# Moving three groups of instructions in the later pairs of a fused attention and gated feed-forward kernel: subtractions on VectorE, copies on ScalarE, one small layer on TensorE

## The chip, the cores and the metric

The kernel runs on one core of one Trainium2 chip. TensorE (PE in the profile) multiplies matrices into PSUM, VectorE (DVE), ScalarE (ACT) and GpSimd (POOL) work element by element, and SyncE (SP) issues most of the transfers between HBM and the on-chip memory SBUF. [...] The metric is the device time of one execution in microseconds (us), as the median of several runs; lower is better.

## The reference

Eight sequences of 512 tokens and 32 states go through a two-way attention, and its output goes through a feed-forward block whose activation is h times cos(h). Everything is float32.

```python
def _attn_ref(x, state):                       # x (8, 8, 512, 64), state (8, 8, 32, 64)
    scale = 1.0 / np.sqrt(D)
    a = softmax(scale * np.matmul(x, state.transpose(0, 1, 3, 2)))
    xread = np.matmul(a, state)
    a2 = softmax(scale * np.matmul(state, x.transpose(0, 1, 3, 2)))
    sread = np.matmul(a2, x)
    return np.concatenate([xread, sread], axis=2)

def _moe_ref(x, w_in, w_out):                  # x (4352, 512), w_in (512, 2048), w_out (2048, 512)
    h = x @ w_in
    g = h * np.cos(h)
    return g @ w_out
```

The row of tokens of a sequence times w_in is never formed as written: since xread is a times state, the kernel first makes state times w_in (the "state products", 32 rows for each head) and then multiplies the attention weights a by that.

## The kernel before, in words

The work is a list of steps, one for each tile of 128 hidden columns: 16 steps (NF) for each of the eight sequences b, and at the end 16 more steps for the states of all sequences together (b = 8, called the states' tiles). Two sequences form a pair of 32 steps (PERIOD). The first pair is placed by a small planner with costs and due times; from step 32 on the order is written out by hand, one call of `later_pair` for each step, and only that part is touched here. Tiles are handled two at a time: an even step and the odd step behind it share one PSUM bank pair `h`.

For a later pair, the hidden tile h of step + 2 is made from the attention weights and the state products with seven half-sized products in place of eight: `seven_part` with k = 0 to 3 (PE, line 543; two parts in each step), sums of weights on POOL made three steps ahead (`sw_sums`, line 521), two copies on ACT after part 0 (`seven_copies`, lines 528 and 529) and two sums on DVE (`seven_sum`, line 551). For the states' tiles the hidden layer is one plain product, `hidden` (PE, line 488, eight matrix instructions). Then comes the activation: `gate` (ACT, line 564, rounds h), `gate2` (DVE, line 567), `gate3` (ACT, line 570, the sine), `gate4` (DVE, line 584, writes g into `g_all` and with that frees the `h` banks for the tile after the next).

The product g times w_out of a pair is likewise done with seven products in place of eight at the outer level, named p1 to p7, and each of these again with seven inner stages (`Product.stage`, k = 0 to 6, PE line 772, eight matrix instructions each). The outer level needs differences between the four quarters of g ("rows" 0 to 3): `outer_sum`, which calls `sub` (line 715) on DVE in pieces of 128x1024 or on POOL in pieces of 128x512. The inner level needs differences too: `Product.sums`, always POOL, also line 715. In an inner product, stage 1 writes the upper half of bank c; its `follow` copies the lower half of c into b and the upper half into a small buffer (ACT, lines 780 and 781). Stage 2 then goes on adding into the lower half of c. Which stages, sums and outer differences belong to which step is laid down in the tables `stage_at`, `sums_at` and `outer_at`; a step has one stage, an even step or the last of a period two, and the 15 states' steps from 129 on share the last 28 stages. In an even step the first of two stages stands in the middle of `later_pair`, the second at the step's end.

The attention of sequence b + 1 and the state products of b and b + 1 are laid into the steps of b by `plan(b)`, as lists `todo[0]` to `todo[5]` for each step s of the 16: `pe` (0), `x_act`, `y_act`, `x_dve`, `y_dve`, `z_act`. `go(n)` issues list n. State products are made in steps s = 0, 3, 8 and 12 (PE, line 312) into the two PSUM banks `at`, and copied out by ACT (`products_kept`, line 462, two copies). In step s = 4 the scores of sequence b + 1 (PE, line 312 again) are written into the same two banks `at`; sequences 3 to 7 have such a step inside the part that is touched.

Below, the pairs are numbered 0 to 3; the outer differences and most inner stages of a pair run in the first half of the pair behind it, those of pair 3 in the states' steps from 128 on.

Of the kernel before, what the change touches and what calls it, by code (L numbers as in the profile page):

```python
# [22 lines left out]
def kernel(  # L23
# [15 lines left out]
    NF = Dff // P  # L39
# [33 lines left out]
    def quad(n):  # L73
        return g_all[:, QT * n:QT * n + QT]
# [392 lines left out]
    def part(b, name, *args):  # L467

        if b not in attn:
            attn[b] = Attention(b)  # L470
        getattr(attn[b], name)(*args)
        if (name, args) == ("reads", (1,)) and b + 1 < B:
            if b > 0:
                attn[b + 1] = Attention(b + 1)
                loads_due.extend(attn[b + 1].load_tokens())
            loads_due.extend(load_x(b + 1))
# [5 lines left out]
    def hidden(t):  # L482
        if t.paired:
            t.hp = h_pairs[t.at][:, t.f % 2, 0:t.n]
        else:
            t.hp = single_pool.tile([P, S], F32, name="h1")
        for i in range(t.kn):
            nc.tensor.matmul(out=t.hp, lhsT=t.lhs(i), rhs=t.rhs(i),  # L488
                             start=(i == 0), stop=(i == t.kn - 1))
# [76 lines left out]
    def gate2(t):  # L566
        nc.vector.tensor_tensor(t.q, t.q.bitcast(I32), t.hp, op=ALU.subtract)  # L567
# [5 lines left out]
    def gate4(t):  # L573
        row = t.row
        if t.i // QT == len(quads_of[row]):
            quads_of[row].append(quads_free.pop(0))
        t.slot = QT * quads_of[row][t.i // QT] + t.i % QT
        t.g = g_all[:, t.slot, 0:t.n]
        g = t.g
        if t.paired:  # L580
            t.mate.slot = t.slot + 1
            t.mate.g = g_all[:, t.slot + 1, 0:t.n]
            g = g_all[:, t.slot:t.slot + 2, 0:t.n]
        nc.vector.tensor_tensor(g, t.hp, t.q, op=ALU.mult)  # L584
# [117 lines left out]
    def fetch_block(n):  # L702

        if n < len(stage_list):
            product_, k = stage_list[n]
            nc.sync.dma_start(
                out=ring[n % NB].rearrange("p i d -> p (i d)"),
                in_=blocks_kept[WEIGHTS[product_.name], ORDER[k]])

    def sub(engine, o, x1, x2):  # L710
        n = max(1, S // o.shape[2])
        if engine is nc.vector:
            n = o.shape[1]
        for i in range(0, o.shape[1], n):
            engine.tensor_tensor(o[:, i:i + n], x1[:, i:i + n], x2[:, i:i + n],  # L715
                                 op=ALU.subtract)
# [253 lines left out]
    warm(WARM, a0.xp[3])  # L970

    def plan(b):
        pe, x_act, y_act, x_dve, y_dve, z_act = [
            {s: [] for s in range(NF)} for _ in range(6)]

        def prod(s, b, nt, *bank):
            pe[s].append((b, "products", nt) + bank)
            x_act[s].append((b, "products_kept", nt) + bank)

        def pairs(s, b, name, kept, i):  # L980
            pe[s] += [(b, name, i), (b, name, i + 1)]
            x_act[s].append((b, kept, i))
            y_act[s].append((b, kept, i + 1))

        def early(b, s):
            for k in range(NK):
                to = (x_dve, y_dve)[k % 2]
                to[s[k // 2]].append((b, "tokens_turned", k))
            pe[s[2]].append((b, "scores"))
            x_dve[s[2]].append((b, "max1"))  # L990
            x_dve[s[3]].append((b, "spread1"))
            y_dve[s[3]].append((b, "shift"))
            y_dve[s[4] - 1].append((b, "max2"))
            z_act[s[4]].append((b, "exps"))
            y_dve[s[4]].append((b, "sums1"))
            x_dve[s[5]].append((b, "spread2"))
            y_dve[s[5]].append((b, "norm1"))

        def late(b, s):
            pairs(s[0], b, "turn", "turn_kept", 0)  # L1000
            pe[s[1]].append((b, "reads", 0))
            pe[s[2]].append((b, "reads", 1))
            x_dve[s[2]].append((b, "keep"))
            pe[s[3]].append((b, "keep2"))
            x_act[s[3]].append((b, "keep3"))

        if b:
            prod(0, b, 1)
            prod(3, b, 2)
            prod(8, b, 3)  # L1010
            if b + 1 < B:
                prod(12, b + 1, 0)
                early(b + 1, (1 + (b == 1), 2 + (b == 1), 4, 5, 7, 8, 9))
                late(b + 1, (9, 10, 11, 15))
        return pe, x_act, y_act, x_dve, y_dve, z_act


    all_tiles = list(tiles())
    for i, t in enumerate(all_tiles):
        t.mate = all_tiles[i ^ 1]  # L1020
    pairs = [all_tiles[2 * NF * n].pair for n in range(B // 2)]
    stage_at, sums_at, outer_at, weights_at = [
        defaultdict(list) for _ in range(4)]
# [25 lines left out]
    dve, pool = nc.vector, nc.gpsimd  # L1049
# [14 lines left out]
    def outer_sum(engine, n, o, x1, x2, half, i):  # L1064
        o, x1, x2 = [quad(quads_of[n, r][half])[:, 2 * i:2 * i + 2]
                     for r in (o, x1, x2)]
        sub(engine, o, x1, x2)
# [29 lines left out]
    def stages(step, n=100):  # L1097
        nonlocal n_stages
        later_copy = step % NF == 7
        copy = nc.vector.tensor_copy if later_copy else nc.scalar.copy  # L1100
        for pd, k in stage_at[step][0:n]:
            pd.stage(k, copy)
            n_stages += 1
            fetch_block(n_stages + NB - 2)
        del stage_at[step][0:n]
# [4 lines left out]
    def go(n):  # L1110
        for p in todo[n]:
            part(*p)
# [513 lines left out]
    def names_raw(i):  # L1626
        h = i % 2
        n = (2 * h, 2 * h + 1) if i < 4 else range(QT)
        return " ".join(f"Q{SLOTS[i]}_{k}" for k in n)

    def later_pair(step, t, ahead):
        coming = ahead[0] if ahead and ahead[0].paired else None
        seven_ = coming is not None and seven(coming)
        first = coming if even or coming is None else coming.mate
        if not t.paired:
            hidden(t)
        if even or not t.paired:
            gate(t)
        else:
            gate3(t.mate)  # L1640
            go(5)
        if seven_:
            seven_part(first, 0 if even else 2)
        elif coming is not None:
            hidden(coming)
        if even or not t.paired:
            gate2(t)
        if t.b == 1 and s in (13, 14):
            halves(2, s - 13)
        if seven_ and not even:  # L1650
            seven_sum(first, 1)
        if not t.paired:
            gate3(t)
        if not t.paired:
            gate4(t)
        elif not even:
            gate4(t.mate)
        if even:
            stages(step, 1)
        go(0)  # L1660
        if not even:
            stages(step, 1)
        if seven_:
            seven_part(first, 1 if even else 3)
            if even:
                seven_sum(first, 0)
        go(1)
        go(3)
        if t.pair is None and not even:
            state_sums(t.mate)  # L1670
            state_sums(t)
        go(2)
        go(4)

    first_pair()
    for step, t in enumerate(all_tiles[FIRST:], FIRST):
        s, even = step % NF, step % 2 == 0
        if s == 0 and t.b < B:
            steps = plan(t.b)
        todo = [p[s] if t.b < B else [] for p in steps]  # L1680
        while stores_due:
            stores_due.pop(0)()
        for u in all_tiles[step + 3:step + 4]:
            if seven(u) and u.f % 2 == 0:
                sw_sums(u)
        now[0] = step
        while totals_due and totals_due[0][0] <= step:
            totals_due.pop(0)[1]()
        if step == PERIOD:
            singles.__exit__(None, None, None)  # L1690
            pool2 = ctx.enter_context(tc.tile_pool(name="hps2", bufs=1,
                                                   space=PSUM))
            h_pairs[0] = pool2.tile([P, 2, S], F32, name="h2")
        later_pair(step, t, all_tiles[step + 2:step + 3])
        if later and later[0][0] <= step:
            later.pop(0)[1]()
        for what in weights_at[step]:
            what()
        for what in outer_at[step]:
            outer_sum(*what)  # L1700
        for pd, k in sums_at[step]:
            pd.sums(k)
        if t.b < B - 1 and t.b > 1 and s in (12, 13):
            halves(t.b + 1, s - 12)
        stages(step)
        load_now(H if step < NF else 4)
        if step == PERIOD * (B // 2) - 8:
            load_end_weights(2)
        if t.pair is None and t.n_th > 3 and len(quads_free) > 2:
            load_end_weights(1)  # L1710
# [36 lines left out]
```

## Time and profile before

| | value |
|---|---|
| time, median of 3 runs | 739.78 us (738.67 to 739.96) |
| the profiled execution's own time | 740.65 us |
| its span, first to last instruction | 738.9 us |
| mean granted TensorE clock | 0.993 |
| DVE busy | 506.8 us (69%) |
| ACT busy | 347.3 us (47%) |
| POOL busy | 542.5 us (73%) |
| DVE line 715, 128x1024, 42 of them | 62.0 us, 1490 ns each |
| POOL line 715, 128x512, 252 of them | 332.5 us, 1349 ns each |

The profile is of one execution. Its own time, 740.65 us, is 0.87 us above the median of the three timed runs, and 1.75 us above its span; a saving that is read from the trace is set against the first of these. Times inside the trace are counted from the first instruction. PE is busy almost throughout, so what counts is its short gaps and what ends them; an idle stretch of another engine matters only where PE waits behind it.

### The profile page before, as it was taken

What the parts mean: (1) busy time and instruction counts of PE and PEld (TensorE: products, weight loads), DVE (VectorE), ACT (ScalarE), POOL (GpSimd) and SP (SyncE); (2) the same over time, 40 slices, a digit from 0 to 9 for tenths busy, and PEclk for the clock granted to TensorE, in tenths of its full rate; (3) what the DMA queues carried; (4) which work ended last, traced back from release to release, by engine and by line L of the source; (5) the groups of instructions that cost most, each with busy time, mean ns of one, the idle gap of its engine ahead of it and who ended that gap; (6) DMA issues with size and microseconds to landing.
All of it is one profiled execution on the core that took longest, in us unless ns stands there. A gap on an engine that the chain in (4) does not pass through costs nothing.

```text
span 738.9 us, 10734 instructions
## 1 busy us (share of the span) xinstructions
PE 708.2 (96%) x3626; PEld 519.0 (70%) x3626; DVE 506.8 (69%) x703; ACT 347.3 (47%) x586; POOL 542.5 (73%) x524
## 2 busy tenths in 40 slices
PE   8898889999999999999999999999999999999997
PEld 3343343477778878777778788777688788888886
DVE  4989979957866668849756577768665467355550
ACT  5799675654463446343634464344634533211110
POOL 1557789375998997588998665879989665799600
PEclk9999999999999999999999999999999999999999
DMA  9966799536346964693238635762225466456662
GB/s 297 285 192 193 236 265 301 122 96 150 87 128 117 214 172 115 142 197 86 82 80 168 160 96 116 147 154 83 75 68 119 115 205 143 108 156 203 155 152 46
DMA packets 204021, 111.33 MB, mean 151 GB/s; under 512 B 149888, under 2 KB 166784, under 8 KB 203968
## 3 DMA queue, kind: packets, MB, share of 16 engines
q1 hardware_dynamic: 202880, 110.14, 57.4%
q8 instruction: 29, 0.48, 0.3%
q10 hardware_dynamic: 960, 0.39, 0.2%
q14 instruction: 24, 0.20, 0.1%
q0 software_dynamic: 128, 0.13, 0.1%
HBM read 87.03 MB, written 23.59 MB: 150 GB/s over the span
## 4 chain that ended last, share of the span: by engine, by line
PE 59%; POOL 21%; DVE 9%; issue 3%; DMA 3%; ACT 2%; SPq 1%; ACTq 0%; POOLq 0%; DVEq 0%
PE o L772 29%; POOL g_all L715 16%; PE h L543 13%; PE h L488 8%; POOL swS_all L521 3%; PE at L312 3%; PE at L877 2%; DMA held<-in_state_dram 2%; PE o L640 2%; POOL sw_all L521 2%; DVE g_all L715 1%; PE at L417 1%; DVE q_all L567 1%; DVE g_all L232 1%; DVE g_all L584 1%
## 5 line engine op out<-in xcount | busy, mean ns | idle before, releaser
L715 POOL TENSOR_TENSOR g_all<-g_all 128x512 f32<-128x512 f32 x252 | 332.5, 1349 | 61.8 <-DVE g_all L715 40.4
L772 PE MATMUL o<-g_all 128*128 128x256 f32 x1456 | 343.7, 381 | 2.4 <-POOL g_all L715 2.4
L772 PEld LDWEIGHTS o<-g_all 128*128 128x128 f32 x1456 | 273.7, 190 | 49.7 <-issue 5.7
L567 DVE TENSOR_TENSOR q_all<-q_all,h 128x1024 f32<-128x1024 int32 (+1 forms) x88 | 85.3, 971 | 40.7 <-ACT q_all L564 40.4
L564 ACT ACTIVATE q_all<-h 128x1024 int32<-128x1024 f32 (+1 forms) x88 | 73.1, 833 | 81.2 <-PE h L543 35.1
L584 DVE TENSOR_TENSOR g_all<-h,q_all 128x1024 f32<-128x1024 f32 (+1 forms) x88 | 85.7, 973 | 24.5 <-ACT q_all L570 23.6
L570 ACT ACTIVATE q_all<-q_all,halfpi 128x1024 f32<-128x1024 f32 (+1 forms) x88 | 84.2, 957 | 38.7 <-DVE q_all L567 38.5
L551 DVE TENSOR_TENSOR h<-h,sums_all 128x256 f32<-128x256 f32 x96 | 41.3, 430 | 77.5 <-PE h L543 60.2
L488 PE MATMUL h<-aT_all,sw_all 128*128 128x512 f32 x128 | 64.0, 628 | 13.0 <-DVE g_all L584 12.3
L543 PE MATMUL h<-aT_all,sw_all 128*128 128x256 f32 x192 | 59.6, 392 | 3.8 <-DVE g_all L584 3.4
L543 PE MATMUL h<-aS_all,swS_all 128*128 128x256 f32 x192 | 60.2, 395 | 2.6 <-ACT sums_all L529 1.8
L715 DVE TENSOR_TENSOR g_all<-g_all 128x1024 f32<-128x1024 f32 x42 | 62.0, 1490 | 0.1
L543 PE MATMUL h<-aS_all,sw_all 128*128 128x256 f32 x192 | 58.0, 384 | 0.1
L488 PEld LDWEIGHTS h<-aT_all,sw_all 128*128 128x128 f32 x128 | 23.2, 195 | 44.3 <-issue 21.5
L521 POOL TENSOR_TENSOR swS_all<-sw_all 128x128 f32<-128x128 f32 x48 | 22.5, 468 | 41.8 <-ACT sw_all L462 41.8
L543 PEld LDWEIGHTS h<-aS_all,swS_all 128*128 128x128 f32 x192 | 33.9, 189 | 27.0 <-issue 12.1
L780 ACT COPY o<-o 128x256 f32<-128x256 f32 x26 | 9.3, 357 | 85.1 <-PE o L772 85.1
L543 PEld LDWEIGHTS h<-aT_all,sw_all 128*128 128x128 f32 x192 | 34.5, 189 | 16.3 <-DVE g_all L584 12.2
L237 POOL TENSOR_TENSOR w_in<-w_in,aS_all 128x1024 int32<-128x1024 int32 (+1 forms) x10 | 22.3, 2241 | 29.9 <-DVE w_in L232 27.2
L787 ACT COPY o<-sums_all 128x256 f32<-128x256 f32 x26 | 9.8, 378 | 68.2 <-PE o L772 68.2
L543 PEld LDWEIGHTS h<-aS_all,sw_all 128*128 128x128 f32 x192 | 35.6, 190 | 8.2 <-DVE h L551 2.7
L607 DVE SCALAR_TENSOR_TENSOR held<-o,held 128x512 f32<-128x512 f32 x38 | 25.9, 681 | 13.7 <-PE o L772 13.1
(116 smaller groups left out, 931.6 us busy)
## 6 DMA issues: line engine op xcount, KB each, us to landing
g_all<-blocks_kept SPq DMA_DIRECT2D x206, 256.0 KB, 2.8
blocks_kept<-g_all SPq DMA_DIRECT2D x48, 256.0 KB, 3.9
g_all<-in_moe_w_out_dram SPq DMA_DIRECT2D x8, 1024.0 KB, 5.7
out_dram<-ot SPq DMA_DIRECT2D x128, 64.0 KB, 2.0
g_all<-in_moe_w_in_dram SPq DMA_DIRECT2D x6, 1024.0 KB, 7.1
x_b<-in_x_dram SPq DMA_DIRECT2D x24, 256.0 KB, 4.7
xT<-in_x_dram SPq DMA_DIRECT2D x80, 64.0 KB, 2.8
x_b<-in_x_dram SPq DMA_DIRECT2D x16, 128.0 KB, 4.3
```

The source lines that it names most:

```text
L237: nc.gpsimd.tensor_tensor(bits, bits, e, op=ALU.add)
L488: nc.tensor.matmul(out=t.hp, lhsT=t.lhs(i), rhs=t.rhs(i), start=(i == 0), stop=(i == t.kn - 1))
L521: nc.gpsimd.tensor_tensor(o, x1, x2, op=op)
L543: nc.tensor.matmul(out=out_, lhsT=w, rhs=r, start=start, stop=True, skip_group_check=True)
L551: nc.vector.tensor_tensor(o, h2[:, LO], sums_all[:, 0], op=ALU.add)
L564: nc.scalar.activation(t.q.bitcast(I32), t.hp, func=ACTF.Copy, bias=0.25)
L567: nc.vector.tensor_tensor(t.q, t.q.bitcast(I32), t.hp, op=ALU.subtract)
L570: nc.scalar.activation(t.q, t.q, func=ACTF.Sin, bias=halfpi, scale=-TWO_PI)
L584: nc.vector.tensor_tensor(g, t.hp, t.q, op=ALU.mult)
L607: nc.vector.scalar_tensor_tensor(out=out.t[:, ch], in0=bank, scalar=TWO_PI, in1=b.t[:, ch], op0=ALU.mult, op1=ALU.add)
L715: engine.tensor_tensor(o[:, i:i + n], x1[:, i:i + n], x2[:, i:i + n], op=ALU.subtract)
L772: nc.tensor.matmul(out=o, lhsT=ring[(self.first + k) % NB][:, i], rhs=g[:, i], start=(start and i == 0), stop=(i == QT - 1), skip_group_ch ...
```

## The change

Three edits, all in steps from 32 on.

The copies of the state products made in an odd step (only s = 3) go into a new list `w_act` of the step behind it and are issued by `go(6)`, which stands after `gate` and `seven_part(first, 0)` with its two copies. They were issued in step s = 3 itself, ahead of the next step's `gate`. This happens once for each of the sequences 2 to 7, in steps 35, 51, 67, 83, 99 and 115 (copies in 36, 52, 68, 84, 100 and 116).

In steps whose next tiles are states' tiles, and whose first two stages are stages 1 and 2 of a product, stage 1 is issued ahead of `hidden`, so that the layer stands between the two stages. It stood ahead of both. This holds in steps 126, 133 and 137.

Outer differences on DVE that read or write row 3 and are due in an even step are kept back in `sums_late` and issued in the odd step behind it, after `gate4`. They were issued at the end of the even step. In each of pairs 0, 1 and 2 this moves one difference of the third step of the half (34, 66, 98) to 35, 67, 99 and one of the fifth (36, 68, 100) to 37, 69, 101; in pair 3 both differences of step 130 go to 131 and one of 132 to 133.

```diff
-        pe, x_act, y_act, x_dve, y_dve, z_act = [
-            {s: [] for s in range(NF)} for _ in range(6)]
+        pe, x_act, y_act, x_dve, y_dve, z_act, w_act = [
+            {s: [] for s in range(NF)} for _ in range(7)]
 
         def prod(s, b, nt, *bank):
             pe[s].append((b, "products", nt) + bank)
-            x_act[s].append((b, "products_kept", nt) + bank)
+            (w_act[s + 1] if s % 2 else x_act[s]).append(
+                (b, "products_kept", nt) + bank)
...
-        return pe, x_act, y_act, x_dve, y_dve, z_act
+        return pe, x_act, y_act, x_dve, y_dve, z_act, w_act
...
+    sums_late = []
+
     def later_pair(step, t, ahead):
...
         if seven_:
             seven_part(first, 0 if even else 2)
         elif coming is not None:
+            if [k for _, k in stage_at[step][0:2]] == [1, 2]:
+                stages(step, 1)
             hidden(coming)
         if even or not t.paired:
             gate2(t)
+        go(6)
         if t.b == 1 and s in (13, 14):
             halves(2, s - 13)
...
         elif not even:
             gate4(t.mate)
+            while sums_late:
+                outer_sum(*sums_late.pop(0))
         if even:
             stages(step, 1)
...
         for what in outer_at[step]:
-            outer_sum(*what)
+            if even and what[0] is dve and 3 in what[2:5]:
+                sums_late.append(what)
+            else:
+                outer_sum(*what)
```

The number of instructions on every engine and every transfer stays the same.

## The prediction

> **What bounds the kernel now.** I read the page first, then the waits of PE behind the first pair, then the chain of waits of one stretch, then the timeline around each gap. From the page, the span and the engines' busy shares, and PE in 40 slices:
>
> ```profile
> span 738.9 us, 10734 instructions
> ...
> PE 708.2 (96%) x3626; PEld 519.0 (70%) x3626; DVE 506.8 (69%) x703; ACT 347.3 (47%) x586; POOL 542.5 (73%) x524
> ...
> PE   8898889999999999999999999999999999999997
> ```
>
> The reader is to see that PE sets the pace; a change can gain only what PE stands idle. The waits of PE from 176 us on (who waited for whom: total, times, longest, in us):
>
> ```profile
> PE h L543 <- DVE g_all L584: 3.4, 8, 0.4
> PE o L772 <- POOL g_all L715: 2.4, 3, 0.8
> PE h L543 <- ACT sums_all L529: 1.8, 4, 0.5
> PE h L543 <- POOL swS_all L521: 0.8, 3, 0.3
> ```
>
> These 8.4 us are nearly all that any reordering can win. But not all of it is free, as the chain of waits of the stretch 332 to 376 us shows (start, length, what):
>
> ```profile
> 333.27 1.12 DVE g_all L715
> ...
> 334.45 6.88 POOL g_all L715 x4
> ...
> 350.43 9.82 POOL g_all L715 x8
> ...
> 362.15 10.84 POOL g_all L715 x8
> ...
> 372.99 0.42 POOL swS_all L521
> ...
> 373.45 0.70 PE h L543 x2
> ```
>
> POOL works here without a break from 334.45 to 373.4 (38.47 us busy of 39.00 in the table of windows), and PE then waits 0.27 us for its sum of weights. The same stretch begins at 176.75 and at 491.96, once for each of pairs 0 to 2. It is started by a difference on DVE in the pair's first step, which isn't moved, so PE can't pass its end earlier than now, however much it saves inside.
>
> [...] the four POOL sums from 334.45 take 6.88 us where four undisturbed ones take 4.96 (at 624.18), and the 128x128 sums at 342.36 and 343.63 take 1.31 and 1.44 us under the DVE pair at 341.91 where 0.46 is usual. So each DVE difference costs POOL about 0.95 us wherever it lies in the stretch. [...]
>
> **The change part by part**, against the profiled execution's 740.65 us.
>
> *States' layer between two stages (steps 126, 133, 137).* The timeline at 623 us:
>
> ```profile
> 623.01 1.89 PE L772 MATMUL o<-g_all 128*128 128x256 f32 x8
> ...
> 624.93 0.36 ACT L780 COPY o<-o 128x256 f32<-128x256 f32 x1 [2.43 <-PE o L772]
> 625.20 0.38 ACT L781 COPY sums_all<-o 128x256 f32<-128x256 f32 x1
> ...
> 625.68 1.97 PE L772 MATMUL o<-g_all 128*128 128x256 f32 x8 [0.78 <-POOL g_all L715]
> ```
>
> Stage 1 ends, ACT copies, and only then stage 2 starts. From start to start the matrix instructions follow at 0.216 us; over this gap it is 1.163, so 0.947 is lost, and another 0.075 at the next one: 1.02 us. It is the same at 661.80 and 681.82. The releaser is named as a POOL sum, but that sum writes what stage 2 doesn't read; the copies end 0.10 us ahead of PE's start, so I take them. Either way `hidden` (8 x 0.216 = 1.73 us of PE) now lies between and covers the 0.8 us of copies. Stage 1 starts 1.73 us earlier: its sums ended at 612.76 (needed 621.3), 651.58 and 673.18 (needed about 658 and 678), and its weights landed 5 us or more before. `hidden` itself comes later, but its banks were freed at 620.88 and its result is read two steps on. The moved orders of DVE (stage 2's sum ahead of other work) and SP (same order) hurt nobody. Gain 3 x 1.02 = 3.06; from below 2.0, if other small waits take a third. I take 3.0. Nothing else stalls PE after 626 us, so it reaches the end.
>
> *Copies behind the seven products, sequences 3 and 5 (steps 52 and 84).* The timeline at 263 us:
>
> ```profile
> 263.27 1.07 ACT L462 COPY sw_all<-at 128x512 f32<-128x512 f32 x2
> ...
> 264.21 1.06 ACT L564 ACTIVATE q_all<-h 128x1024 int32<-128x1024 f32 x1
> ...
> 265.13 0.41 ACT L528 COPY h<-h 128x256 f32<-128x256 f32 x1
> ...
> 265.57 0.37 ACT L529 COPY sums_all<-h 128x256 f32<-128x256 f32 x1
> 265.64 0.18 PEld L312 LDWEIGHTS at<-xT,st_all 64*32 64x32 f32 x16 [0.33 <-ACT h L528]
> ```
>
> The scores at 265.64 overwrite the two banks that the copies read. With the gate first: gate 263.27 to 264.2, the two copies of h to 265.0, then the two moved copies, the second ending at about 265.97. The second score instruction goes to that bank, so PE waits to about 266.1 (0.14 us from an ACT end to PE's start, as at 581.02 to 581.16): 0.47 us lost, and behind the waiting PE stands all of the step. PE had no wait near here that the earlier gate could remove, and POOL has idle time until the next pair, so nothing takes it back. Two steps: +0.94; bounds 0.6 and 1.4 (0.3 and 0.7 each).
>
> *The same, sequence 7 (step 116).* No scores follow, and here PE did wait for the copy of h:
>
> ```profile
> 580.65 0.37 ACT L529 COPY sums_all<-h 128x256 f32<-128x256 f32 x1
> ...
> 581.16 0.67 PE L543 MATMUL h<-aS_all,swS_all 128*128 128x256 f32 x2 [0.38 <-ACT sums_all L529]
> ```
>
> The copy ends 0.94 us earlier, and the loss of 0.54 us (start to start) is gone: -0.5; bounds -0.54 and 0.
>
> *The same, sequences 2, 4 and 6, with DVE's differences (steps 34 to 37, 66 to 69, 98 to 101).* The difference at 338.11 (2.09 us, part of it waiting for POOL) leaves the place ahead of gate4, which then ends at about 340.1 where it ended at 341.99; PE's loss of 0.28 at 342.05 goes. Three differences in a row follow gate4, and gate2 behind them starts at 344.1 to 344.7 as before. The moved copies then end at about 344.72, and the scores, due at 344.56, wait 0.26. The difference at 348.65 moves behind gate4, which ends 0.97 earlier; the loss of 0.59 at 352.23 goes. Together PE would be 0.6 us ahead. But it then waits at the sum of weights of 373.40, behind the unbroken POOL stretch, into which the same three differences fall with the same 0.95 us each. [...] So the 0.27 of idle time there becomes about 0.8, and three pairs give 3 x -0.1 = -0.3; bounds +0.2 and -0.6 each.
>
> *Differences of pair 3 (steps 130 and 132).* DVE has gaps of 1 to 5 us there and POOL's sums are used 5 us or more after they end: 0.
>
> Sum: -3.0 + 0.94 - 0.5 - 0.3 = -2.9, say -2.8 for small waits: 737.85 for a profiled execution. The profiled one lay 0.87 above the median, so on the median 739.78 - 2.8 = 737.0 us.
>
> **The rivals.**
>
> *POOL gives way (chance 0.13).* If POOL's stretch shortens, because the regrouped differences cost it less or its start comes earlier, the 0.6 us in each of three pairs count: 737.0 - 3 x 0.5 = 735.5. For it: PE's present wait is only 0.27. [...]
>
> *The layer's place brings nothing (0.10).* Stage 1, pulled forward, or `hidden`, pushed back, finds a wait of its own, and the 3.0 stays lost: 740.0. For it: the releaser named is POOL. Against: the inputs' ends above, and the sum named starts with stage 1's first instructions, so it moves with it.
>
> *Scores wait much longer (0.06; slower).* One mechanism: the copy at line 528 needs part 0 of the seven products, which needs gate4's banks; if that is late, both moved copies and the scores behind them are late too. Its price is w in each of five steps, less the 0.9 us that POOL's wait can hide in three of them: 2w + 3(w - 0.9) against the 3.8 gained elsewhere. It decides from w = 1.3; with two copies and a gate in full, w = 2.1, it gives 739.78 + 7.8 - 3.8 = 743.8. Against: at 263 us part 0 ends at 263.6, before the gate does.
>
> **How the numbers follow.** My forecast holds 0.71, with its own range 736.0 to 738.4. The range of all reaches down to 735.3 for the first rival and up to 738.8 for dear scores and a cheap layer. A measurement tells apart about 0.2%, 1.5 us. Faster: forecast and first rival, less a few hundredths in which the small costs all fall badly, 0.82; within: the second rival and that rest, 0.11; slower 0.07.
>
> **What would show it.** In the new trace: no gap between stages 1 and 2 in the three states' steps, eight instructions of line 488 between them; 0.4 to 0.6 us of idle PE ahead of the scores in steps 52 and 84; no wait for line 584 in steps 36 and 38, and PE's wait for the sum of weights in steps 42, 74 and 106 grown from 0.27 to about 0.8. If that last wait is gone, POOL wasn't the limit. If PE waits ahead of stage 1 or of `hidden` in the states' steps, the largest term is wrong.

## The result, and the profile after it

The changed kernel takes 743.02 us (median of 5 runs, 741.52 to 743.44), the kernel before, run beside it, 739.78 us: ratio 1.0041, 95% interval 1.0024 to 1.0058. It is slower by about 3 us, where 2.8 us less were forecast. The profiled execution took 743.28 us. Its page, span and PE:

```profile
span 741.5 us, 10731 instructions
...
PE 709.5 (96%) x3626; PEld 523.0 (71%) x3626; DVE 508.7 (69%) x703; ACT 347.7 (47%) x586; POOL 539.8 (73%) x524
...
PE   8898889999999999999999999999999999999897
```

One slice has changed: the third from the right, 686 to 704 us, has dropped from 9 to 8. The waits of PE from 176 us on (who waited for whom: total, times, longest):

```profile
PE o L772 <- issue: 3.6, 1, 3.6
...
PE h L543 <- DVE h L551: 3.5, 6, 0.7
PE h L543 <- DVE g_all L584: 2.1, 5, 0.4
PE h L543 <- POOL swS_all L521: 0.8, 3, 0.3
```

The three waits of 0.8 us of line 772 for line 715 are gone, as forecast: the layer covers them. In their place stands one wait of 3.6 us, longer than the three together. "Issue" says that the view saw no engine that PE waited for, so the timeline around the gap has to be read. The changed kernel:

```profile
675.00 3.62 PE L772 MATMUL o<-g_all 128*128 128x256 f32 x16
...
678.45 1.89 PE L488 MATMUL h<-st_all,w_in 128*128 128x256 f32 x8
678.51 2.51 POOL L824 TENSOR_TENSOR held<-held 128x512 f32<-128x512 f32 x2
678.65 0.36 ACT L780 COPY o<-o 128x256 f32<-128x256 f32 x1 [3.14 <-PE o L772]
678.92 0.38 ACT L781 COPY sums_all<-o 128x256 f32<-128x256 f32 x1
...
680.18 1.89 PE L772 MATMUL o<-g_all 128*128 128x256 f32 x8
...
680.97 9.86 POOL L715 TENSOR_TENSOR g_all<-g_all 128x512 f32<-128x512 f32 x8
...
682.17 0.42 DVE L783 TENSOR_TENSOR sums_all<-o,sums_all 128x256 f32<-128x256 f32 x1 [5.87 <-PE o L772]
682.52 10.11 DVE L849 TENSOR_TENSOR g_all<-g_all 128x128 f32<-128x128 f32 x8
...
692.55 0.68 DVE L567 TENSOR_TENSOR q_all<-q_all,h 128x512 f32<-128x512 int32 x1
693.15 0.70 DVE L615 STREAM_TRANSPOSE ot<-held 128x512 f32<-128x512 f32 x1
...
693.78 0.40 DVE L789 TENSOR_TENSOR o<-o,sums_all 128x256 f32<-128x256 f32 x1
...
694.27 3.65 PE L772 MATMUL o<-g_all 128*128 128x256 f32 x8 [3.58 <-issue]
```

In step 137 the layer (line 488, at 678.45) now stands between stage 1, the second half of the group at 675.00, and stage 2 at 680.18, with no gap. Stage 2 starts behind the second copy, which ends at 679.30, and ahead of POOL's sums at 680.97, so it doesn't need the sum that the view of the kernel before names as its releaser. PE's group at 694.27 is stage 6 of product p7 in step 139. It starts 0.10 us after the sum of stage 4 (line 789) has ended on DVE, and PE's last group before it ended at 690.7. That sum stands on DVE behind a gate, a transposition, and the eight state differences of step 137 (line 849, called by `state_sums`: differences of g for the products of the states at the very end). What it reads from PE was written by 690.7, and it starts at 693.78, after all of these. The differences take 10.11 us, and nearly all of it is the first one:

```profile
L849 DVE TENSOR_TENSOR g_all<-g_all x32: 267/284/8456, 682.5 to 715.8; 128x128 f32<-128x128 f32 x32
```

(Shortest, median and longest in ns.) 8,456 ns is the first of step 137, from 682.52 to 690.97; the median is 284. The trace shows no idle time of DVE before it and names no engine that it waited for. What stands beside it is POOL, with sums without a break until 690.83. The kernel before, same place:

```profile
678.06 2.48 POOL L824 TENSOR_TENSOR held<-held 128x512 f32<-128x512 f32 x2
678.20 7.24 DVE L849 TENSOR_TENSOR g_all<-g_all 128x128 f32<-128x128 f32 x8
...
680.30 1.89 PE L772 MATMUL o<-g_all 128*128 128x256 f32 x8
...
681.48 10.00 POOL L715 TENSOR_TENSOR g_all<-g_all 128x512 f32<-128x512 f32 x8 [0.94 <-PE o L772]
...
685.36 0.41 DVE L783 TENSOR_TENSOR sums_all<-o,sums_all 128x256 f32<-128x256 f32 x1
```

There POOL stopped for 0.94 us, because its next sum overwrites what PE's stage 1 of step 137 (from 680.30 on) still read. In that stop the first difference got in (2.50 us after its start), and the rest followed, some at 0.28 us and some at 1.24 to 1.35 us in turn with POOL's sums. In the changed kernel the same stage 1 starts at 676.72, 3.6 us earlier: 1.7 because it stands ahead of `hidden`, the rest gained at the two layers before. POOL comes 0.45 us later (line 824 at 678.51 in place of 678.06). So it finds its buffer free and doesn't stop.

The wait has a tail. The changed kernel by stretches (length, then busy time and number of instructions of PE, weight loads, DVE, ACT and POOL, granted clock, DMA):

```profile
690.63:694.27 3.64, 0.07 (x1) 0.03 (x1) 3.57 (x12) 0.72 (x1) 0.20 (x1) 1.00 0.00 0
694.27:698.20 3.93, 3.92 (x11) 3.19 (x12) 3.86 (x11) 0.60 (x1) 1.26 (x1) 0.57 0.71 121
```

Over the 3.93 us behind the gap of 3.58 us the granted TensorE clock was 0.57, and the eight matrix instructions there take 3.65 us where 1.89 is usual. Over the 3.95 us behind a gap of 1.45 us (the kernel without the layer's edit, below) it was 1.00. The loss is 3.58 + 1.76 = 5.3 us.

For the experiments two stretches of each trace are compared, since what lies ahead of them, with the first loads, alone takes from 165.2 to 168.8 us in these traces. The *middle* goes from the first state products of line 312 after 160 us to the last (step 124), the *tail* from there to the first product of the states (line 877), behind which all kernels take 28.2 us. Each ratio is to the kernel before as it ran beside that kernel, with a median of 739.49 to 740.53 us; so kernels are compared by their ratios, not by their medians.

| kernel | median us | ratio to before, 95% interval | middle | tail |
|---|---|---|---|---|
| before | 739.78 | | 430.53 | 112.65 |
| changed | 743.02 | 1.0041, 1.0024 to 1.0058 | 430.88 | 115.10 |
| layer alone | 742.71 | 1.0032, 1.0021 to 1.0044 | 430.57 | 115.11 |
| without the layer's edit | 742.82 | 1.0030, 1.0019 to 1.0041 | 431.32 | 114.35 |
| the same, pair 3's differences kept | 740.09 | 1.0002, 0.9993 to 1.0011 | 431.71 | 112.66 |
| layer in two steps of three | 747.71 | 1.0081, 1.0056 to 1.0105 | 430.91 | 119.34 |
| changed, differences held to step 139 | 738.94 | 0.9978, 0.9969 to 0.9987 | 430.79 | 111.18 |
| changed, POOL made to stop | 738.23 | 0.9974, 0.9965 to 0.9982 | 431.02 | 111.09 |
| changed, differences on POOL | 739.53 | 0.9995, 0.9986 to 1.0004 | 430.80 | 111.42 |
| changed, differences held to step 141 | 736.84 | 0.9964, 0.9952 to 0.9975 | 431.68 | 109.87 |
| selected parts, held to step 141 | 736.82 | 0.9952, 0.9938 to 0.9967 | 429.94 | 109.87 |

### The profile page after: what moved, and what is told of

Its sections match the earlier page's. It is cut to its first block, busy times and chain, and to the rows that moved or that the text cites. A ratio compares the mean times of both kernels' runs of the same rounds, so it can differ in the third digit from the quotient of the medians.

```text
span 741.5 us, 10731 instructions
## 1 busy us (share of the span) xinstructions
PE 709.5 (96%) x3626; PEld 523.0 (71%) x3626; DVE 508.7 (69%) x703; ACT 347.7 (47%) x586; POOL 539.8 (73%) x524
## 4 chain that ended last, share of the span: by engine, by line
PE 56%; POOL 25%; DVE 9%; issue 4%; DMA 3%; ACT 2%; SPq 1%; POOLq 0%; DVEq 0%; ACTq 0%
PE o L772 27%; POOL g_all L715 19%; PE h L543 13%; PE h L488 6%; POOL swS_all L521 4%; PE at L312 3%; PE at L877 2%; PE o L640 2%; DMA held<-in_state_dram 2%; DVE g_all L715 1%; PE at L417 1%; DVE q_all L567 1%; DVE g_all L232 1%; DVE g_all L584 1%; PE o L877 1%
## 5 line engine op out<-in xcount | busy, mean ns | idle before, releaser
L715 DVE TENSOR_TENSOR g_all<-g_all 128x1024 f32<-128x1024 f32 x42 | 58.7, 1419 | 0.1
L521 POOL TENSOR_TENSOR swS_all<-sw_all 128x128 f32<-128x128 f32 x48 | 25.4, 530 | 45.4 <-ACT sw_all L462 45.4
L462 ACT COPY sw_all<-at 128x512 f32<-128x512 f32 x48 | 25.8, 591 | 18.5 <-PE at L312 18.3
```

The source lines that it names most:

```text
L462: (copy or nc.scalar.copy)(sw_of[self.b, nt][:, j, c0:c1], to[j][:, c0:c1])
L521: nc.gpsimd.tensor_tensor(o, x1, x2, op=op)
```

## The experiments

**Which edit makes the wait.** The layer's edit alone on the kernel before, and the change without it.

```diff
+            if [k for _, k in stage_at[step][0:2]] == [1, 2]:
+                stages(step, 1)
```

> Only the edit of the states' layer, in steps 126, 133 and 137. Theory A (the layer's edit wins about 1.0 us at each of three places and loses about 5.5 us later, where PE waits for DVE's state differences behind stage 2's sum): 739.8 - 3.1 + 5.5 = 742.2 us, and the long wait of PE near 690 us is there. Rival B (the loss comes from the moved copies or the outer differences, which shift everything that follows): 736.7 us and no wait of PE over 1 us behind 600 us.

Measured: 742.71 us, tail 115.11 as in the changed kernel, first state difference 8.48 us, PE's wait 3.60. As theory A had it: this edit by itself makes the tail as long as the whole change does.

> The moved copies and outer differences without the layer's edit. Theory A: the waits of PE grow by 0.65 and 0.55 us at the scores of sequences 3 and 5, one of 0.6 us goes for sequence 7, and the pairs' POOL stretches swallow the rest: 739.8 + 0.2 = 740.0 us, with the three waits of 0.78 us in the states' steps back and no long one. Rival B: most of the 3.2 us of the whole change, 742.5 us or more.

Measured: 742.82 us, a miss. Without the layer's edit the three waits of 0.8 us are back and the long one is gone, but there is another. The timeline:

```profile
678.00 11.22 DVE L849 TENSOR_TENSOR g_all<-g_all 128x128 f32<-128x128 f32 x8
...
681.28 10.29 POOL L715 TENSOR_TENSOR g_all<-g_all 128x512 f32<-128x512 f32 x8 [0.18 <-PE o L772]
...
689.65 0.67 PE L772 MATMUL o<-g_all 128*128 128x256 f32 x2 [1.45 <-POOL g_all L715]
```

POOL's stop has shrunk from 0.94 to 0.18 us. The first difference gets in only there (3.25 us after its start), one more follows at once, and each of the other six waits for a POOL sum; together they take 11.22 us where the kernel before had 7.24, and PE waits 1.45 us. So other parts of the change move POOL against PE too. I had thought the tail untouched without the layer.

**Is it the place of stage 2's sum on DVE?** In the changed kernel line 783 runs ahead of the state differences, in the kernel before behind them. With the layer left as before in step 137 alone, that order is the old one.

```diff
-            if [k for _, k in stage_at[step][0:2]] == [1, 2]:
+            if [k for _, k in stage_at[step][0:2]] == [1, 2] and step != 137:
```

> The whole change, but the layer stands between stages 1 and 2 in steps 126 and 133 alone, not in 137. Theory A (only step 137 puts DVE's stage sum ahead of the state differences): 739.8 + 0.2 - 2 x 1.02 = 738.0 us, no long wait. Rival C (stage 1 pulled forward costs at each of the three places): 741 to 742 us, a long wait left.

Measured: 747.71 us. Every theory missed. The timeline:

```profile
674.45 16.29 DVE L849 TENSOR_TENSOR g_all<-g_all 128x128 f32<-128x128 f32 x8
...
676.63 2.53 POOL L824 TENSOR_TENSOR held<-held 128x512 f32<-128x512 f32 x2
679.07 9.87 POOL L715 TENSOR_TENSOR g_all<-g_all 128x512 f32<-128x512 f32 x8
...
690.67 0.41 DVE L783 TENSOR_TENSOR sums_all<-o,sums_all 128x256 f32<-128x256 f32 x1
```

The first difference comes while POOL has eleven more instructions to run behind the current one. It takes 14.64 us, until POOL stops, and PE waits 6.5 us. The order of line 783 is not the cause, and neither is the moved stage of step 137 as such: here the two layers moved earlier have already brought PE forward, and POOL's stop is gone without it. What this kernel, the changed one and the layer alone have in common is that POOL doesn't stop there. One of the nine executions took 739.54 us, the others 745.66 to 748.08; the trace is of the one with 745.66, and what was different in the quick one isn't shown.

**Take the differences away from there.** First held back to step 139, behind whose differences POOL has little left:

```diff
-    sums_late = []
+    sums_late, held_back = [], []
...
-            state_sums(t.mate)
-            state_sums(t)
+            held_back.extend((t.mate, t))
+            while held_back and step != 137:
+                state_sums(held_back.pop(0))
```

> The whole change with one addition: the eight state differences of step 137 are issued with those of step 139. Theory A (DVE's queue is held by the state differences, which wait for POOL's sums): the long wait of PE is gone and all three gains stay, 739.8 + 0.2 - 3.1 = 736.9 us; the sixteen differences take some 5 us in all. Rival D (PE's long wait is for something else of that stretch, a sum on POOL or a weight transfer): 742 us or more, the wait still there.

Measured: 738.94 us, faster than before (0.9969 to 0.9987), but only about half of what was expected. The long wait is gone. What is left of the gain goes into this:

```profile
703.81 2.40 PE L772 MATMUL o<-g_all 128*128 128x256 f32 x10 [1.35 <-DMA g_all<-blocks_kept]
```

The weights of the next stages are fetched on SP behind four stores, and these wait for the transposition of line 615, which now stands on DVE behind sixteen differences in a row (4.84 us) and ends at 698.2.

**Stop POOL, and nothing else.** This tells whether POOL's unbroken row is the cause or only a companion. One POOL instruction of a single column, behind the differences of step 137 and reading the last of them; in POOL's queue it comes after the second of the eight sums.

```diff
             state_sums(t)
+            if step == 137:
+                nc.gpsimd.tensor_tensor(swS_all[:, 0, 0, 0:1],
+                                        t.x[:, 0:1], rows_of[t.f + NH].x[:, 0:1],
+                                        op=ALU.subtract)
```

> The whole change, and behind the eight state differences of step 137 one POOL subtraction of a single column that reads the last of them and writes a buffer not used any more; in POOL's queue it stands behind the second of the eight sums from 680.97 on, so POOL has to stop there until the eight differences are done. Theory A (POOL's unbroken queue keeps DVE out): the first difference takes about 1 us instead of 8.46, all eight are done by about 686, PE's wait of 3.6 us and the half pace behind it are gone; from the first state products after 160 us to the end it takes 574.15 - 5.4 = 568.8 us, the time is about 737.5 to 738. Rival B (something else holds the difference until 690.97): nothing changes, 743. Rival C (POOL's sums, 2 to 3 us later, are now what PE waits for): the long wait goes, but one for line 715 takes its place.

```profile
682.63 2.76 DVE L849 TENSOR_TENSOR g_all<-g_all 128x128 f32<-128x128 f32 x8
...
685.47 0.19 POOL L1681 TENSOR_TENSOR swS_all<-g_all 128x1 f32<-128x1 f32 x1 [1.88 <-DVE g_all L849]
685.62 7.46 POOL L715 TENSOR_TENSOR g_all<-g_all 128x512 f32<-128x512 f32 x6
...
702.43 7.15 PE L772 MATMUL o<-g_all 128*128 128x256 f32 x32 [1.25 <-DMA g_all<-blocks_kept]
```

POOL stops for 1.88 us, and the eight differences take 2.76 us in place of 10.11. The long wait is gone, and 738.23 us is 2.6 per mille less than before. An added instruction made the changed kernel about 5 us faster (ratio 0.9974 to before in place of 1.0041). A wait for a weight fetch of 1.25 us remains, so the tail is 111.09 and not the 109.9 of a tail without it. With the same differences computed by POOL:

```diff
-    def state_sums(t):
+    def state_sums(t, engine):
...
-            nc.vector.tensor_tensor(o, x1, x2, op=ALU.subtract)
+            engine.tensor_tensor(o, x1, x2, op=ALU.subtract)
...
-            state_sums(t.mate)
-            state_sums(t)
+            e = nc.gpsimd if step == 137 else nc.vector
+            state_sums(t.mate, e)
+            state_sums(t, e)
```

> The whole change, with the eight state differences of step 137 computed by POOL instead of DVE. DVE has no subtraction of SBUF data left between POOL's sums there. Theory A: the DVE queue runs free, PE's wait of 3.6 us is gone, POOL's sums behind end 8 x 0.46 = 3.7 us later, which nobody waits for: 568.8 us for the stretch to the end, time about 737.5 to 738. Rival B (the wait for DVE in step 139 has another cause than the differences): it stays, 743.

Measured: 739.53 us, tail 111.42. The starvation is gone here too, and the fetch is 1.6 us late. In times no gain over before can be told (0.9986 to 1.0004): its 22 runs scatter from 737.35 to 743.27 us, and the trace, 1.2 us shorter than before in the tail, is of the fastest of them. What the slower ones lose, no trace shows.

**When is DVE kept out?** Rows of POOL subtractions (128x512) alone, and DVE subtractions with both inputs in SBUF that come into them. The core of it, shortened (each of the three programs below ran once):

```python
for i in range(a, a + n):
    nc.gpsimd.tensor_tensor(g[:, i], e_all[:, 0, 0:S], e_all[:, 1, 0:S], op=sub)
    if i == a + j - 1:
        nc.scalar.copy(mid, g[:, i])         # releases DVE behind sum j
nc.vector.tensor_tensor(d_all[:, k, 0:w], e_all[:, 1, 0:w], e_all[:, 0, 0:w], op=sub)
```

> Leaves the reference's whole computation out: a row of stretches in which POOL runs eight 128x512 subtractions of SBUF data and DVE, from the second of them on, has one subtraction of SBUF data of width 128, 256, 512 or 1024, then four of 128, then three of 1024, and then the same with POOL sums that each read the one before. Theory A (a waiting DVE subtraction isn't served between POOL instructions that stand ready in POOL's queue): in the stretches of independent POOL sums each first DVE subtraction ends only after the eighth sum, so it takes about 6 x 1.25 = 7.5 us or more whatever its width; where each POOL sum waits for the one before, it is let in after one, 1 to 2 us. Theory B (only small ones are passed over): 128 wide takes over 7 us, 1024 wide about 2 us as at 338.11 in the kernel before. Theory C (DVE is served after the POOL instruction that runs): all take 1 to 2.3 us, and the 8.46 us of the changed kernel have another cause.

With rows of eight, theory C: each of the DVE subtractions, of 128 to 1024 columns, was let in after the one POOL sum that ran (0.56 to 1.49 us for the first of a row). That excluded a plain "DVE waits behind whatever POOL has queued". In the traces of the whole kernels POOL had already run a long row when the kept-out ones came, so the next rows were of 24.

> Leaves the reference's whole computation out: stretches of 24 POOL subtractions (128x512, SBUF) without a break, and three DVE subtractions of SBUF data that come when 18, 8, 16, 2, 12, 15, 20 and 18 of the sums are done; they are 128 wide, in the third stretch 1024 and in the last 256. In the traces so far a DVE subtraction was let in after the POOL instruction that ran wherever POOL had at most 10 instructions without a break behind it, and was passed over by 2 to 11 where it had 14 to 26. Theory A (a long unbroken POOL queue shuts DVE out until POOL stops): behind 8 and 2 sums the first takes about 1.2 us, behind 14 and more it ends only with the 24th, so about 6 us behind 18 and 9 behind 15, at 1024 wide too. Theory B (it's the width): 128 wide behind 18 takes over 5 us, 1024 behind 16 about 2 us. Theory C (it needs something of the kernel that is not here): all of them are let in after one sum, 0.5 to 2.3 us.

The timeline of DVE, three subtractions in each group; 18, 8, 16, 12 and 15 POOL sums ran without a break ahead of the one they met:

```profile
30.71 7.06 DVE L82 TENSOR_TENSOR d_all<-e_all 128x128 f32<-128x128 f32 x3
...
49.07 3.09 DVE L82 TENSOR_TENSOR d_all<-e_all 128x128 f32<-128x128 f32 x3
...
89.10 12.30 DVE L82 TENSOR_TENSOR d_all<-e_all 128x1024 f32<-128x1024 f32 x3
...
147.85 3.10 DVE L82 TENSOR_TENSOR d_all<-e_all 128x128 f32<-128x128 f32 x3
...
181.78 10.72 DVE L82 TENSOR_TENSOR d_all<-e_all 128x128 f32<-128x128 f32 x3
```

Theory A. Behind 8 and 12 sums the first took 0.56 us. Behind 15, 16 and 18 it took 10.32, 10.03 and 6.66 us and ended with the row, at 1024 columns as at 128. The three groups that aren't shown fit: behind 2 sums 0.56 us; behind 20, and behind 18 at 256 columns, 4.22 and 6.79 us and to the end of the row. Is it time or number?

> Leaves the reference's whole computation out: four stretches of POOL subtractions without a break, each with one or two 128x128 DVE subtractions of SBUF data: 32 sums of width 128 with the difference behind 24 of them (about 11 us of POOL's time), 12 of width 1024 with the difference behind 8 (about 19 us), 20 of 512 with differences behind 6 and 17, and 20 of 512 with one behind 17 while DVE does small PSUM sums behind the third, sixth, ninth, twelfth and fifteenth. Before, a difference behind 14 sums of 512 was let in and one behind 15 (18 us) was not. Theory A (the number of POOL instructions without a break decides): the first difference is shut out until POOL stops, the second let in after one sum. Theory B (the time for which POOL runs without a break decides, some 18 us): the other way round. In the third stretch the difference behind 17 is let in if a difference that got in starts the count anew (A and B both), and shut out if not; in the fourth it is shut out if it is POOL's run that counts, and let in if it is DVE's idle time before it.

```profile
18.37 2.87 DVE L82 TENSOR_TENSOR d_all<-e_all 128x128 f32<-128x128 f32 x1
...
40.50 1.88 DVE L82 TENSOR_TENSOR d_all<-e_all 128x128 f32<-128x128 f32 x1
...
58.10 0.80 DVE L82 TENSOR_TENSOR d_all<-e_all 128x128 f32<-128x128 f32 x1
...
71.57 0.80 DVE L82 TENSOR_TENSOR d_all<-e_all 128x128 f32<-128x128 f32 x1
...
97.06 3.24 DVE L82 TENSOR_TENSOR d_all<-e_all 128x128 f32<-128x128 f32 x1
```

The number. Behind some 25 short sums (10 us of POOL) it was kept out for 2.87 us, to the end of the row; behind 8 long ones (19 us of POOL) it came in after the running one (1.88 us). In the third row the subtraction behind 17 sums came in (0.80 us), where another had come in behind 6; in the fourth, without that one, it was kept out to the end of the row (3.24 us), though DVE did five small PSUM sums on the way. (The "behind 14 sums" of the expectation is the third subtraction of the group at 147.85, which followed two that had got in.) So in these four rows the outcome went with the number of POOL's instructions without a break, counted from the last DVE subtraction that got in, and not with their time. The traces of the whole kernels give the same border. The table has POOL's instructions ahead of the one that DVE met, counted in the traces since POOL last stood idle, and in brackets since DVE last got in, where that was later:

| trace | DVE subtraction | POOL ahead | it ends |
|---|---|---|---|
| before | 128x1024 at 657.64 | 10 (3) | after the running sum (2.15 us) |
| rows of 24 | 128x128 at 147.85 | 12 | after the running sum (0.56 us) |
| layer in two steps of three | 128x128 at 674.45 | 14 | after 11 more, when POOL stops (14.64 us) |
| without the layer's edit | 128x128 at 678.00 | 19 (14) | after 2 more, when POOL stops (3.25 us) |
| before | 128x128 at 678.20 | 26 (15) | after 1 more, when POOL stops (2.50 us) |
| changed | 128x128 at 682.52 | 19 | after 6 more, when POOL stops (8.46 us) |
| changed, differences on POOL | 128x128 at 689.09 | 6 | after the running sum (0.75 us) |

In the last line a gap of 0.08 us in POOL's row is taken for idle time; counted from the gap before that, of over 1 us, it would be 31. No other subtraction of the kept traces goes against the border. Why it lies there, no run shows.

**What moves POOL when the layer isn't moved.** The change without the layer's edit, and with pair 3's outer differences where they were:

```diff
-            if even and what[0] is dve and 3 in what[2:5]:
+            if (even and what[0] is dve and 3 in what[2:5]
+                    and step < PERIOD * 4):
```

> The change without the layer's edit, and the outer differences moved for pairs 0 to 2 alone; those of pair 3 (steps 130 and 132) stay in the even steps. Theory A (the 1.45 us for which PE waits in step 138 without the layer's edit comes from the three differences of pair 3 that moved, which take POOL's stop ahead of the state differences from 0.94 to 0.18 us): the wait is gone, from the last state products to the end it takes about 28.2 + 112.65 = 140.8 us as in the kernel before, and the time is 740.5 + 0.8 = 741.3 less what step 116 gains, so about 741. Rival B (the loss comes from PE's other position, copies and pairs 0 to 2): the wait of over 1 us stays, 742.8.

```profile
679.56 7.28 DVE L849 TENSOR_TENSOR g_all<-g_all 128x128 f32<-128x128 f32 x8
...
682.85 10.04 POOL L715 TENSOR_TENSOR g_all<-g_all 128x512 f32<-128x512 f32 x8 [0.91 <-PE o L772]
```

Theory A: the stop is 0.91 us again, the differences take 7.28, the tail is 112.66. The three moved differences of pair 3 had cost POOL 0.73 us against PE, and the tail 1.7 us.

**The whole change and a selection, with the differences two steps later still**, in step 141 behind that step's own (POOL's eight sums end at 689.6 here, ahead of step 141):

```diff
-    sums_late = []
+    sums_late, held_back = [], []
...
-            state_sums(t.mate)
-            state_sums(t)
+            if step == 137:
+                held_back.extend((t.mate, t))
+            else:
+                state_sums(t.mate)
+                state_sums(t)
+            while held_back and step == 141:
+                state_sums(held_back.pop(0))
```

> The whole change, with the eight state differences of step 137 issued in step 141 behind that step's own, as in the best version. Theory A: everything that was forecast stays, the starvation goes and so does the wait of 1.3 us for a weight fetch that the other repairs kept, since no differences stand ahead of the store's transposition in step 139: 574.15 - 5.4 = 568.8 us from the first state products after 160 us to the end, and 737.0 to 737.5 in time. Rival B (the wait for the fetch comes from the moved copies and outer differences): 570.1 us and about 738.3, as where POOL was stopped.

Measured: 736.84 us, and neither long wait is left: the tail is 109.87, 2.78 less than before. (Its whole stretch, 569.73, is longer than A said: the middle has a wait of 0.6 us for a transfer at 252.8 us in this execution, which the changed kernel's doesn't have.) The selection leaves out the moved outer differences and moves the copies in step 116 alone:

```diff
-            x_act[s].append((b, "products_kept", nt) + bank)
+            (w_act[s + 1] if s % 2 and b == B - 1 else x_act[s]).append(
+                (b, "products_kept", nt) + bank)
...
```

> The kernel before with the layer between stages 1 and 2, the copies behind the seven products in step 116 alone (not in steps 36 to 100), the outer differences where they were, and the eight state differences of step 137 issued in step 141 behind that step's own. Theory A: the layer's 3.06 and step 116's 0.5 to 0.6 are gained and nothing is lost, so from the first state products after 160 us to the end 571.37 - 3.6 = 567.8 us against 571.37, and about 736.5 to 737 in time. Rival B (holding the differences back makes a wait at the end, for the 24 differences in a row or for the stores and fetches behind them on SP, as in the held variant of step 139): 738 to 739.

Measured: 736.82 us (736.34 to 737.11, 6 runs) beside 740.12, ratio 0.9952, interval 0.9938 to 0.9967: faster than both kernels. Its waits of PE from 176 us on:

```profile
PE h L543 <- DVE g_all L584: 3.4, 8, 0.4
PE h L543 <- ACT sums_all L529: 1.4, 3, 0.5
PE h L543 <- POOL swS_all L521: 0.8, 3, 0.3
```

These are the kernel before's, without line 772 and with one wait for line 529 less. Middle -0.59, tail -2.78.

## Why the prediction was wrong

*The layer between two stages.* The step that failed is the sentence "The moved orders of DVE (stage 2's sum ahead of other work) and SP (same order) hurt nobody", with "Nothing else stalls PE after 626 us, so it reaches the end". Its own term was right: the three gaps are gone, and where DVE isn't starved the tail gains 2.78 us (twice) for the 3.0 taken. But it was PE's being late that made POOL stop at 681 us in the kernel before, and the prediction gave that 0.94 us of idle POOL no thought. It was the place at which the DVE differences got in. Without it the first of them took 8.46 us and held up the sum of stage 4 behind it. The wait that replaced it costs 5.3 us; 5.3 - 2.8 = 2.5 is the tail's measured 115.10 - 112.65.

*What DVE and POOL cost each other.* "So each DVE difference costs POOL about 0.95 us wherever it lies in the stretch" is the same gap in the reasoning: an estimate from two places of one trace, it prices what DVE does to POOL and not what POOL does to DVE. That a DVE difference which comes second waits for one POOL instruction at most was my estimate, from their mean of 1349 ns; 8.46 and 14.64 us were measured. The trace of before held a warning: the first difference at 678.20 took 2.50 us, more than one POOL instruction, and nothing waited for it.

*Copies in steps 52 and 84*: forecast +0.47 each, with the scores waiting for the moved copies. PE's place in the changed trace against before moves by +0.65 and +0.54 us there, and the scores of sequence 3 take 1.74 us in place of 1.09. *Step 116*: forecast -0.5, measured -0.62. *Pairs 0 to 2*: forecast -0.1 each (my estimate), measured -0.12, -0.15 and -0.12. The sum of these was +0.14 by the forecast and is +0.18 in the trace; the middle stretch is 0.35 longer, since one group of line 772 at 412 us starts later by 0.16, which six of the seven other traces with the same middle don't show (their middles lie between 430.79 and 431.71). So these terms were right to 0.2 us. In the pairs the way there was only half right. PE gets about 0.7 us ahead and the end of the stretch takes that back, as said, and three waits for line 584 are gone; but the wait for the sum of weights stayed at 0.3 us. The time went into six new waits of up to 0.7 us for DVE's sums of line 551 (at 357.91 us, for one, after DVE has worked without a break from the moved difference at 351.51 on; and at 371.57, close ahead of the sum of weights).

*Differences of pair 3*: forecast 0. Measured without the layer's edit: 1.7 us, by the same starvation. "DVE has gaps of 1 to 5 us there" looked at the steps where they were put, not at the POOL row that they push on.

None of the rivals had this. The slower one, a long wait of the scores, didn't come about.

*The late fetch.* Of the repairs, three kept a wait of PE for weights, and two didn't. The traces show the chain: the transposition of line 615 stands on DVE behind the differences, SP's four stores wait for it, and the fetch stands on SP behind the stores. Counted in us from PE's first instruction of `hidden` in step 139; PE reaches the stage that needs the weights 13.98 us after it:

| kernel | transposition starts | fetch issued | it lands | PE waits |
|---|---|---|---|---|
| before | 6.89 | 9.96 | 13.42 | 0 |
| selected parts, held to step 141 | 6.89 | 9.95 | 12.94 | 0 |
| changed, POOL made to stop | 8.07 | 11.14 | 15.09 | 1.25 |
| changed, differences held to step 139 | 8.75 | 11.82 | 15.19 | 1.35 |
| changed, differences on POOL | 9.41 | 12.48 | 15.43 | 1.59 |

The transposition is late where the differences ahead of it take longer. Where POOL is stopped or computes the differences itself, its other sums come later and the second eight differences, in step 139, alternate with them: 4.17 and 5.51 us in place of 2.98.

What stays open: why DVE is kept out from some number of POOL instructions on, what the slower executions lose where POOL computes the differences, and the one quick execution of the layer in two steps of three.

## What to carry to other kernels

An idle stretch of an engine that has time to spare can be what lets another engine work (here 0.94 us of POOL): before a change that makes PE earlier, ask which engine stopped because PE was late, and what ran in that stop. Where DVE subtractions with two SBUF inputs meet a long row of POOL's, put them where the row has ended (here in step 141 in place of 137: ratio to before 0.9964 in place of 1.0041), or give POOL a break by an instruction that waits for them (0.9974). An instruction whose time is several times its median (here 2.50 us against 0.285 in the kernel before), though nothing waits for it yet, is the place to look at first.

## What the runs showed of the hardware

All of this is of DVE subtractions with both inputs in SBUF (float32) that came while POOL worked on SBUF data, in the traces kept here. POOL's instructions are those ahead of the running one, counted since POOL last stood idle or DVE last got in.

Where at most 12 had run, the DVE subtraction was let in after the running one: 0.56 us behind 2, 8 and 12 sums in the rows of 24, 2.15 us for the 128x1024 one at 657.64 in the kernel before. Where it was 14 to 25, it waited until POOL stopped: 14.64 us behind 14 (layer in two steps of three), 10.32, 10.03 and 6.66 us behind 15, 16 and 18 (rows of 24), 8.46 us behind 19 (changed), 2.87 us behind some 25 (short sums). 13 was not met. The time and width of the sums didn't decide it: some 25 of 128 columns, 10 us of POOL, shut it out, and 8 of 1024 columns, 19 us, didn't (1.88 us).

DVE subtractions that followed each other closely took turns with POOL's sums: in the kernel before three of the eight 128x128 differences took 1.24 to 1.35 us each beside them, where 0.28 is usual.
